# The start of a delta-rule attention and SwiGLU kernel: the first two Gram products, square roots, masks and weight staging rearranged

## The chip, the cores and the metric

The kernel runs on one core of one Trainium2 chip. The metric is the device time of one execution in microseconds (us). Three executions of the kernel before took 696.74, 697.48 and 697.67 us, so the median is 697.48 us. One further execution was profiled. It took 695.99 us, and its span, from the first to the last instruction, is 693.9 us.

## The reference

The input is q, k and v of 4 batches, 8 heads, 768 tokens and 48 values a head, and a scalar beta for every token and head. The first half is a delta-rule recurrence, the second a SwiGLU feed-forward block:

```python
k_n = k / (norm(k, axis=-1) + 1e-06)
for t in range(768):
    y[t]   = q[t] @ state
    v_old  = k_n[t] @ state
    state += beta[t] * outer(k_n[t], v[t] - v_old)
x   = y as (3072 tokens, 384)           # heads side by side
g   = x @ w_gate                        # 384 -> 1536
out = (g * sigmoid(g) * (x @ w_val)) @ w_out   # 1536 -> 384
```

The three weight matrices arrive as 64-bit floats, and are made into 32-bit ones on the chip.

## The kernel before

The recurrence is worked in 12 chunks of 64 tokens. In each chunk, the part that goes through the chunk's own tokens is a triangular system, whose inverse Z comes from the chunk's products K K^T, the norms of k and beta. The kernel makes the inverses for two chunks at a time; the first pair, chunks 0 and 1, has code of its own (the names with `first_`). Four batches are in the tiles as two halves of the 128 partitions, heads as even and odd (`par`).

The start goes so, in the order in which it is written (the order is by hand, each engine works its list from the front, and nothing overtakes on an engine):

- `norms` (VectorE) squares and sums k for chunks 0 and 1. The square root of chunk 0 is a `pow` on GpSimd (L392). For chunk 1, `second_norms` makes it with twelve small VectorE instructions (L399 to L422).
- `turned` transposes k on TensorE, ScalarE copies the result back, and `first_gram` forms K K^T: for chunk 0 in 32 products (L671), for chunk 1 in 64 smaller ones (L677, L678). `first_diag` gathers the 32 by 32 blocks of the diagonal, `spread_beta` brings beta to the rows (L452, L459), `first_scale` multiplies by beta over the square of the norm, partly on GpSimd (L714 to L716), and `first_substitution` inverts by 30 short VectorE instructions (L734, L740). `spread_z` (L757, L759) writes Z where the products read it: for chunk 0 on VectorE and ScalarE, for chunk 1 on GpSimd.
- `gram_steps` makes the products of q and k. For chunks 0 and 1 they are copied by ScalarE and then masked on GpSimd (L566), four instructions of 128x512.
- `stage` loads a piece of the weights. A piece of the first kind is 128 rows by 256 columns of w_gate or w_val, 256 KB. If it is given `after`, GpSimd first copies one column of the earlier piece into the new place (L266), and the load on the SP queue (L267) waits for that copy. So a load starts only when the earlier piece has landed and when GpSimd has come to the copy. Pieces 2 to 13 are held by the piece two before, 14 to 22 by the piece three before. GpSimd's list has the copies of pieces 2 to 5, then the four masks, the two `spread_z` of chunk 1, and then the copies from piece 6 on.
- `power_step` (ScalarE, L279 and L285) and `convert` (VectorE, L296, L304, L316) make the 32-bit weights from a piece that has landed. Both stand in the engines' lists among the work of the attention.
- `first_advance` does the recurrence for chunk 0, `advance(1)` for chunk 1, interleaved with the first feed-forward products by `chain`. `gate_val` (L1477) multiplies by w_gate and w_val: the columns f = 0, 2, 4, 6 (in units of 128, two at a time) for chunk 0, then the same for chunk 1, and so on. f = 0 needs pieces 0 to 5, f = 2 pieces 6 to 11, f = 4 pieces 12 to 17, f = 6 pieces 18 to 23.
- The SP queue holds all loads of this part in one order: q, k, v of the first chunks, pieces 0 to 5, v of chunk 1 (L185), pieces 6 to 22, v of chunk 2, k of chunk 4 (L139), piece 23, and so on.

From chunk 2 on, the feed-forward products go by a scheme with fewer multiplications (L1317, L1594); that part is the same before and after. `unread` issues products whose result nobody reads (L661).

## Time and profile before

| what | before |
|---|---|
| time, median of 3 (lowest, highest) | 697.48 us (696.74, 697.67) |
| time of the profiled execution | 695.99 us |
| its span | 693.9 us |
| TensorE matmul busy | 656.0 us, 95% of the span |
| VectorE, ScalarE, GpSimd busy | 473.2, 255.4, 206.7 us |
| mean granted clock of TensorE | 0.992 |

The span begins with the first instruction, and 2.1 us of the profiled time lie outside it. In rows of instructions ("the timeline") the columns are the start in us, the length from the first start to the last end in us, the engine, the line, the operation, what it writes and reads, the shape and the count; in brackets stands the idle time of the engine just before, and what ended it. PE is TensorE, PEld its weight loads, DVE VectorE, ACT ScalarE, POOL GpSimd, SPq the issue of DMAs by the SP queue. One fp32 product makes two rows of PE and two of PEld, a "pair" each. "issue" means that the engine waited for nothing that the profile shows. In rows of waits the columns are the total in us, the number and the longest. The chain of waits lists start, length and work, following back from the last instruction of the span.

### The profile page before, as it was taken

The page shows a single profiled execution, that of the slowest core. Times are in us where ns is not written, and L with a number is a line of the kernel's source. Part 1 is how long each engine was busy: PE and PEld are TensorE (multiplying, and loading weights), DVE is VectorE, ACT ScalarE, POOL GpSimd, SP SyncE. Part 2 cuts the span into 40 slices and gives each one's busy share as a digit, 9 for nine tenths or more (in the row PEclk, how much of TensorE's full clock was granted, in tenths as well). Part 3 has the DMA queues.
Part 4 walks back from the last instruction along what each step waited for, and adds up shares of the span by engine and source line. Part 5 has one row for each costly group of instructions (what it writes and reads, how often), then busy time and mean ns, then how long its engine had stood idle before and what let it go on. Part 6 is the DMA issues. An engine that isn't in the chain of part 4 may idle for free.

```text
span 693.9 us, 24970 instructions
## 1 busy us (share of the span) xinstructions
PE 656.0 (95%) x10914; PEld 604.4 (87%) x10914; DVE 473.2 (68%) x986; ACT 255.4 (37%) x545; POOL 206.7 (30%) x320
## 2 busy tenths in 40 slices
PE   7877899999899999999999999999999999999997
PEld 4666788856798899999999999999999999999997
DVE  6887478898669956757756757756757755645463
ACT  3876476303532343244233244233222333142130
POOL 6332021203786030783030783030783000000000
PEclk9999899999999999999999999999999999999999
DMA  9645926005314462068172077152077232132220
GB/s 138 159 119 163 258 91 205 1 24 90 97 26 122 113 142 78 19 136 178 39 154 78 14 142 177 37 132 79 15 153 155 64 94 78 40 93 77 70 76 24
DMA packets 147437, 68.57 MB, mean 99 GB/s; under 512 B 123456, under 2 KB 126560, under 8 KB 147328
## 3 DMA queue, kind: packets, MB, share of 16 engines
q1 hardware_dynamic: 144992, 66.48, 40.0%
q8 instruction: 86, 1.41, 0.9%
q10 hardware_dynamic: 2080, 0.39, 0.4%
q14 instruction: 23, 0.19, 0.1%
q0 software_dynamic: 256, 0.10, 0.1%
HBM read 59.08 MB, written 7.86 MB: 96 GB/s over the span
## 4 chain that ended last, share of the span: by engine, by line
PE 75%; DVE 12%; DMA 4%; SPq 3%; issue 2%; POOL 2%; ACT 1%; DVEq 0%; POOLq 0%; ACTq 0%
PE ffn L1317 38%; PE ffn L1594 17%; PE ffn L1477 9%; DMA h_f<-in_moe_w_val_dram 2%; PE p_px L1110 1%; SPq L139 1%; DVE zb L616 1%; DVE x_t L610 1%; PE p_py L527 1%; PE p_py L1164 1%; PE p_px L1091 1%; SPq L185 1%; DVE x_t L1547 1%; PE p_py L1189 1%; PE p_py L1081 1%
## 5 line engine op out<-in xcount | busy, mean ns | idle before, releaser
L1317 PE MATMUL ffn<-x_t,w_gv 128*128 128x128 f32 x760 | 101.5, 277 | 6.7 <-DVE x_t L1544 6.7
L1317 PEld LDWEIGHTS ffn<-x_t,w_gv 128*128 128x128 f32 x760 | 92.3, 192 | 8.4 <-issue 6.1
L1594 PE MATMUL ffn<-wo_sb,h_f 128*128 128x192 f32 x480 | 84.2, 329 | 0.6 <-ACT ffn L1586 0.6
L850 POOL TENSOR_TENSOR n_b<-mb,half 128x32 f32<-128x32 f32 x5 | 27.6, 5526 | 182.2 <-DVE mb L581 182.2
L1317 PE MATMUL ffn<-x_ffn,w_gv 128*128 128x128 f32 x600 | 79.2, 275 | 0.0
L1594 PEld LDWEIGHTS ffn<-wo_sb,h_f 128*128 128x128 f32 x480 | 77.8, 190 | 1.6 <-ACT ffn L1586 0.9
L1353 ACT ACTIVATE sil<-ffn 128x256 f32<-128x256 f32 x95 | 34.6, 382 | 114.9 <-PE ffn L1317 107.0
L616 POOL TENSOR_TENSOR zb<-zb,h_f 128x31 f32<-128x31 f32 (+15 forms) x124 | 72.4, 584 | 9.7
L610 POOL TENSOR_TENSOR h_f<-zb,mb 128x31 f32<-128x31 f32 (+15 forms) x124 | 69.9, 563 | 14.4 <-DVE mb L598 5.0
L1317 PEld LDWEIGHTS ffn<-x_ffn,w_gv 128*128 128x128 f32 x600 | 73.0, 192 | 0.0
L1317 PE MATMUL ffn<-x_t,h_f 128*128 128x128 f32 x464 | 63.6, 280 | 4.2 <-DVE ffn L1544 3.9
L1354 DVE TENSOR_TENSOR h_f<-sil,ffn 128x256 f32<-128x256 f32 x95 | 37.6, 418 | 42.8 <-ACT sil L1353 42.8
L1317 PEld LDWEIGHTS ffn<-x_t,h_f 128*128 128x128 f32 x464 | 56.3, 192 | 6.2 <-DVE ffn L1544 4.9
L1477 PE MATMUL ffn<-x_ffn,w_gv 128*128 128x256 f32 x216 | 48.0, 381 | 0.0
L1477 PEld LDWEIGHTS ffn<-x_ffn,w_gv 128*128 128x128 f32 x216 | 40.7, 190 | 5.6
L1547 DVE TENSOR_TENSOR o_sb<-o_sb,ffn 128x192 f32<-128x192 f32 x49 | 17.1, 349 | 31.4 <-PE ffn L1594 31.0
L1594 PE MATMUL ffn<-last_k,h_f 128*128 128x192 f32 x200 | 35.9, 327 | 0.0
L1477 PE MATMUL ffn<-x_t,w_gv 128*128 128x256 f32 x144 | 35.0, 393 | 0.7 <-DVE x_t L1058 0.7
L1547 DVE TENSOR_TENSOR ffn<-ffn,p_sb 128x512 f32<-128x512 f32 x36 | 24.7, 693 | 16.0 <-PE ffn L1317 14.9
L1594 PEld LDWEIGHTS ffn<-last_k,h_f 128*128 128x128 f32 x200 | 32.8, 190 | 0.2 <-DVE o_sb L1547 0.2
L1477 PEld LDWEIGHTS ffn<-x_t,w_gv 128*128 128x128 f32 x144 | 27.2, 196 | 5.0 <-ACT x_t L1058 0.9
L1317 PE MATMUL ffn<-x_ffn,h_f 128*128 128x128 f32 x224 | 30.0, 277 | 0.0
(351 smaller groups left out, 1178.8 us busy)
## 6 DMA issues: line engine op xcount, KB each, us to landing
h_f<-w_s SPq DMA_DIRECT2D x81, 256.0 KB, 2.8
more_w<-w_s SPq DMA_DIRECT2D x27, 256.0 KB, 2.8
vin<-in_v_dram SPq DMA_DIRECT2D x48, 96.0 KB, 3.5
out_dram<-o_sb SPq DMA_DIRECT2D x48, 96.0 KB, 2.2
kn<-in_k_dram SPq DMA_DIRECT2D x20, 192.0 KB, 4.7
w_s<-h_f SPq DMA_DIRECT2D x10, 256.0 KB, 2.7
zt<-in_moe_w_out_dram SPq DMA_DIRECT2D x6, 384.0 KB, 5.4
qpad<-in_q_dram SPq DMA_DIRECT2D x36, 64.0 KB, 2.9
```

The lines of the kernel that those rows point to most:

```text
L139: dmas[b % len(dmas)].dma_start(out=t[64 * b : 64 * b + 64, :, :, 0:D].rearrange("p bp h d -> p (bp h) d"), in_=halves(x, c, b).rearrange( ...
L185: nc.sync.dma_start(out=vin[c][s : s + 64, par].rearrange("p bp j d -> p (bp j) d"), in_=src[par],)
L527: nc.tensor.matmul(p_v[par][half_of(b if of_q else b ^ par), bp, j], kt[c][half_of(par), bp, j, b], xt[half_of(par), bp, j, b],)
L610: engine.tensor_tensor(out=t_v, in0=zb[:, 0 : j + 1, j : j + 1].to_broadcast([128, j + 1, m]), in1=mb[:, j : j + 1, j + 1 : R].to_broadcas ...
L616: engine.tensor_tensor(out=zb[:, 0 : j + 1, j + 1 : R], in0=zb[:, 0 : j + 1, j + 1 : R], in1=t_v, op=ALU.add,)
L850: nc.gpsimd.tensor_tensor(out=n, in0=mb.rearrange("p j i -> p (j i)")[:, 0 : R * R : R + 1], in1=half, op=ALU.pow,)
L1317: nc.tensor.matmul(p[:, u], w(u), moving, start=start and u == 0, stop=True, skip_group_check=True,)
L1353: nc.scalar.activation(silu_of, p[:, 0:2], ACTF.Silu)
L1354: nc.vector.tensor_tensor(out=h_of(c, PAIRS[r][e % 3], e // 3), in0=silu_of, in1=p[:, 2:4], op=ALU.mult)
L1477: nc.tensor.matmul(ps[name][:, i], w_sb[:, t, (f + i) * 128 : (f + i + 1) * 128], xts[c][:, t], start=(t == 0 and i == 0), stop=(t == KT - 1),
L1547: nc.vector.tensor_tensor(out=out, in0=a, in1=b, op=ALU.add)
L1594: nc.tensor.matmul(p[x, part], a(f - f % 2)[:, f % 2], b(f), start=not begun and f == 0, stop=f == FH - 1, skip_group_check=True,)
```

## The change

- The square root of chunk 1 is now a second `pow` on GpSimd; the twelve VectorE instructions are gone. `first_n` squares the reciprocal, so that beta is multiplied once, on VectorE, and the sign goes into two `scalar_tensor_tensor` of `first_scale`. The transposition of the diagonal blocks stands before `first_n`, not behind it.
- `first_gram` does chunk 1 in 32 products like chunk 0, and `first_diag` combines its two halves like those of chunk 0: two scaled copies on ScalarE and two instructions on VectorE.
- GpSimd's masks of chunk 0 stand between the copies of pieces 6 and 7 and of pieces 7 and 8. The masks of chunk 1 go to VectorE, into the fourth and fifth step of `chain`. Z of chunk 1 is spread by VectorE (first half) and ScalarE (second half) inside `first_advance`.
- Pieces 6 to 9 are held by the piece two before, 10 to 17 by the piece three before, and 18 to 22 by none.
- In `first_advance` the transpositions of y stand before the products for the state. The conversions of pieces 0, 2 and 4 and the power steps of 0, 2, 4 and 1 stand one step of `first_advance` earlier or later than before.

The order of the SP queue is the same before and after. Of the diff, only the body of the removed function is cut:

```diff
@@ -387,39 +387,8 @@
             nc.vector.tensor_reduce(
                 out=n[:, par], in_=ksq_v[:, par], axis=mybir.AxisListType.X, op=ALU.add
             )
-        if c == 0:
-            n = n_t[0][:, c]
-            nc.gpsimd.tensor_tensor(out=n, in0=n, in1=half[:, 0:HH], op=ALU.pow)
-
-    def second_norms():
-
-        n = n_t[0][:, 1]
...
-        nc.vector.tensor_tensor(out=n, in0=n, in1=x, op=ALU.mult)
+        n = n_t[0][:, c]
+        nc.gpsimd.tensor_tensor(out=n, in0=n, in1=half[:, 0:HH], op=ALU.pow)
 
     def divide_beta(g, r_n):
         for _ in range(2):
@@ -463,6 +432,7 @@
         nc.vector.tensor_scalar_add(n, n, 1e-6)
         r_n = work.tile([128, R], FP32, name="r_n", tag="n_b", bufs=1)
         nc.vector.reciprocal(r_n, n)
+        nc.vector.tensor_tensor(out=r_n, in0=r_n, in1=r_n, op=ALU.mult)
         r_b = work.tile([128, R], FP32, name="r_b", tag="nb", bufs=1)
         nc.vector.transpose(r_b, r_n)
         return r_b
@@ -559,8 +529,8 @@
         if of_q and c < 2:
             for par in range(2):
                 to = p_sb[c][:, par].rearrange("p bp j i -> p (bp j) i")
-                under_mask(nc.gpsimd, to, to)
-            yield
+                under_mask(nc.gpsimd if c == 0 else nc.vector, to, to)
+                yield
 
     def under_mask(engine, to, of):
         engine.tensor_tensor(
@@ -663,28 +633,16 @@
     def first_gram(c, tag):
 
         p_v = [p.rearrange("p (x h i) -> p x h i", x=2, i=R) for p in banks("p_g", tag)]
-        half_rows = C
         for bp, j, par, b, _ in every():
             k_v = kt[c][half_of(par), bp, j, b].rearrange("p (x i) -> p x i", x=2)
-            h = NJ * bp + j
-            if c == 0:
-                nc.tensor.matmul(
-                    p_v[par][half_of(b), :, h], kt[c][half_of(par), bp, j, b], k_v
-                )
-                continue
-            hi, lo = QUADS[2 * b][0], QUADS[2 * b + 1][0]
-            twice = k_v[:, 0:1].to_broadcast([half_rows, 2, R])
-            nc.tensor.matmul(p_v[par][hi, :, h], k_v[:, 0], twice)
-            nc.tensor.matmul(p_v[par][lo, :, h], k_v[:, 1], k_v)
+            nc.tensor.matmul(
+                p_v[par][half_of(b), :, NJ * bp + j], kt[c][half_of(par), bp, j, b], k_v
+            )
         return p_v
 
     def first_diag(c, p):
         to = first_of["diag"][:, HH * c : HH * c + HH]
         to = to.rearrange("p (par h) j -> p par h j", par=2)
-        if c > 0:
-            for par in range(2):
-                nc.scalar.copy(to[:, par], p[par][:, 1])
-            return
         for par in range(2):
             nc.scalar.mul(to[:, par], p[par][:, 0], m_rows[:, 3:4])
         for par in range(2):
@@ -709,16 +667,19 @@
 
     def first_scale(r_b):
         zb, b = first_of["zb"], beta_b[:, 0]
-        nb = sil[:, 0, 0:R]
-        for _ in range(2):
-            nc.gpsimd.tensor_tensor(out=b, in0=b, in1=r_b, op=ALU.mult)
-        nc.gpsimd.tensor_scalar_mul(nb, b, -1.0)
+        nc.vector.tensor_tensor(out=b, in0=b, in1=r_b, op=ALU.mult)
         nc.gpsimd.tensor_copy(zb[:, 0 : R * R : R + 1], b)
         mb = pairs_of_blocks(first_of["mb"])[:, :, :, 0:B16]
-        nb = nb.rearrange("p (b i) -> p b i", b=2)[:, :, None, :]
-        nc.vector.tensor_tensor(
-            out=mb, in0=mb, in1=nb.to_broadcast([128, 2, B16, B16]), op=ALU.mult
-        )
+        for x in range(2):
+            at = slice(B16 * x, B16 * x + B16)
+            nc.vector.scalar_tensor_tensor(
+                out=mb[:, x],
+                in0=mb[:, x],
+                scalar=-1.0,
+                in1=b[:, None, at].to_broadcast([128, B16, B16]),
+                op0=ALU.mult,
+                op1=ALU.mult,
+            )
 
     def first_substitution():
 
@@ -1028,6 +989,7 @@
                 lambda par, b, j: t[there(par, b), 1 - par, bp, j],
             )
             plus(uu[:, :, bp], t[:, 1:3, bp], pairs[bp])
+        spread_z(1, 0, nc.vector)
         load_v(2)
         yield
         y = work.tile([128, NB, NJ, 2, D], FP32, name="y", tag="r", bufs=2)
@@ -1042,7 +1004,6 @@
             copy(y[:, bp, :, 0], pairs[bp][:, 0])
             for b in range(2):
                 copy(y[half_of(b), bp, :, 1], pairs[bp][half_of(1 - b), 1])
-        p_s = of_state(0, uu)
         yield
         y_f = y.rearrange("p bp j par d -> p bp (j par d)")
         xts[0] = x_first
@@ -1056,6 +1017,8 @@
                 at = slice(k * 128, (k + 1) * 128)
                 nc.tensor.transpose(p_f[bp][:, k], y_f[:, bp, at], ident)
             copy(x_v[:, :, bp], p_f[bp])
+        p_s = of_state(0, uu)
+        spread_z(1, 1, nc.scalar)
         nc.scalar.copy(state, p_s)
         yield
 
@@ -1865,14 +1828,13 @@
         turned(0, False, 0)
         p_g = [first_gram(0, "px")]
         first_diag(0, p_g[0])
-        second_norms()
         turned(1, False, 2)
         p_g.append(first_gram(1, 2))
         first_diag(1, p_g[1])
         spread_beta(copy_a)
         turned(0, True, 0)
+        nc.vector.transpose(first_of["mb"][:, 0 : R * R], first_of["flat"])
         r_b = first_n()
-        nc.vector.transpose(first_of["mb"][:, 0 : R * R], first_of["flat"])
         first_scale(r_b)
         for n in range(6):
             stage(n, n - 2 if n > 1 else None)
@@ -1899,32 +1861,35 @@
         spread_z(0, 1, nc.vector, others)
         scale_v(0)
         next(first_q[1])
-        power_step(0)
-        next(first_q[1])
+        stage(6, 4)
         next(first_q[0])
-        for x in range(2):
-            spread_z(1, x, nc.gpsimd)
-        for n in range(6, 14):
+        stage(7, 5)
+        next(first_q[0])
+        for n in range(8, 10):
             stage(n, n - 2)
-        for n in range(14, 23):
+        for n in range(10, 18):
             stage(n, n - 3)
+        for n in range(18, 23):
+            stage(n)
         zb_1 = work.tile([128, R, R], FP32, name="zb", bufs=1)
         new_nt(0, spare_of_q, state.rearrange("p b bp j d -> p (b bp j d)")[:, 0:512])
         new_nt(1, zb_1.rearrange("p k i -> p (k i)"), spare_of_q[:, 0:512])
         gens["advance", (0,)] = [first_advance(), 0]
         step("advance", advance, 0)
+        power_step(0)
+        step("advance", advance, 0)
         converts_first(0)
-        step("advance", advance, 0)
-        step("advance", advance, 0)
         power_step(2)
         step("advance", advance, 0)
         converts_first(2)
-        step("advance", advance, 0)
         power_step(4)
         step("advance", advance, 0)
         step("advance", advance, 0)
+        power_step(1)
+        step("advance", advance, 0)
+        step("advance", advance, 0)
         converts_first(4)
-        for n in (1, 3, 5):
+        for n in (3, 5):
             power_step(n)
         scale_v(1)
         converts_first(1)
@@ -1941,6 +1906,8 @@
             step("advance", advance, 1)
             n, ahead = ((1, 7), (2, 6), (4, 4))[len(went)] if len(went) < 3 else (2, 4)
             went.append(n)
+            if len(went) in (4, 5):
+                next(first_q[1])
             convert(todo[:n], ahead)
             del todo[:n]
```

More of the change, by code (lines that the diff above doesn't have):

```diff
@@ L389, in norms @@
             )
-        if c == 0:
-            n = n_t[0][:, c]
-            nc.gpsimd.tensor_tensor(out=n, in0=n, in1=half[:, 0:HH], op=ALU.pow)
-    def second_norms():
-        n = n_t[0][:, 1]
-        x = work.tile([128, HH], FP32, name="x", tag="n_b", bufs=1)
-        t = work.tile([128, HH], FP32, name="t", tag="nb", bufs=1)
-        nc.vector.tensor_scalar(
-            out=words(t),
-            in0=words(n),
-            scalar1=1,
-            scalar2=None,
-            op0=ALU.logical_shift_right,
-        )
-        nc.vector.tensor_scalar(
-            out=words(x),
-            in0=words(t),
-            scalar1=-1.0,
-            scalar2=float(0x5F3759DF),
-            op0=ALU.mult,
-            op1=ALU.add,
-        )
-        for _ in range(3):
-            nc.vector.scalar_tensor_tensor(
-                out=t, in0=x, scalar=-0.5, in1=n, op0=ALU.mult, op1=ALU.mult
-            )
-            nc.vector.tensor_tensor(out=t, in0=t, in1=x, op=ALU.mult)
-            nc.vector.scalar_tensor_tensor(
-                out=x, in0=t, scalar=1.5, in1=x, op0=ALU.add, op1=ALU.mult
-            )
-        nc.vector.tensor_tensor(out=n, in0=n, in1=x, op=ALU.mult)
+        n = n_t[0][:, c]
+        nc.gpsimd.tensor_tensor(out=n, in0=n, in1=half[:, 0:HH], op=ALU.pow)
     def divide_beta(g, r_n):
```

2 lines of the change are left out of this document (removed).

## The prediction

> **What bounds the kernel now.** I read the busy time by stretches first, then the chain of waits, then the timeline of each engine up to 90 us. The stretches have, behind the window, the busy time of PE, PEld, DVE, ACT and POOL, then the granted clock, the DMA share and GB/s.
>
> ```profile
> 60.00:70.00 10.00, 6.43 (x147) 5.31 (x147) 7.06 (x21) 6.93 (x18) 1.15 (x5) 0.89 0.66 201
> 70.00:80.00 10.00, 6.93 (x30) 6.08 (x30) 4.47 (x14) 4.58 (x11) 0.00 (x0) 0.77 1.05 227
> 80.00:90.00 10.00, 10.00 (x166) 8.72 (x165) 7.15 (x14) 6.67 (x13) 0.00 (x0) 1.00 1.02 326
> 90.00:100.00 10.00, 10.00 (x48) 8.81 (x47) 4.92 (x7) 9.91 (x15) 0.00 (x0) 1.00 0.01 3
> ```
>
> TensorE is the bound of the whole. From 80 us on it is busy without a hole (10.00 of 10), but between 60 and 80 us 13.4 of 20, at a lower clock. What the start saves before 78 us therefore moves the end one for one. These are the holes of TensorE:
>
> ```profile
> 62.88 1.56 PE L1477 MATMUL ffn<-x_t,w_gv 128*128 128x256 f32 x6
> 68.00 1.54 PE L1189 MATMUL p_py<-ident,y 128*128 128x128 f32 x6 [3.56 <-ACT y L1179]
> 69.34 2.40 PE L1477 MATMUL ffn<-x_t,w_gv 128*128 128x256 f32 x6
> 74.81 1.94 PE L511 MATMUL p_px<-ident,kn 128*128 128x128 f32 x8 [3.07 <-DVE zt L296]
> 78.16 5.35 PE L1477 MATMUL ffn<-x_t,w_gv 128*128 128x256 f32 x24
> ...
> 121.83 1.04 PE L511 MATMUL p_px<-ident,kn 128*128 128x128 f32 x8
> ```
>
> There is one of 3.56 us ahead of the transpositions of y, and one of 3.07 us ahead of those of k of chunk 4. The rows around them are slow: six products of L1477 take 2.40 us where they took 1.56, and two lots of eight transpositions fill 74.81 to 78.16, where one lot takes 1.04 later. What held them is in ScalarE's and SP's rows:
>
> ```profile
> 62.20 0.45 ACT L279 ACTIVATE w_gv<-wo_sb 128x256 f32<-128x256 f32 x1
> 65.38 0.43 ACT L279 ACTIVATE w_gv<-wo_sb 128x256 f32<-128x256 f32 x1 [2.40 <-DMA wo_sb<-in_moe_w_gate_dram]
> 66.51 0.47 ACT L1177 COPY y<-p_py 128x384 f32<-128x384 f32 x1
> 66.99 0.96 ACT L1179 COPY y<-p_py 64x384 f32<-64x384 f32 x2
> ...
> 29.05 0.33 SPq L267 DMA_DIRECT2D h_f<-in_moe_w_gate_dram  x1
> 31.27 2.64 SPq L185 DMA_DIRECT2D vin<-in_v_dram  x4
> 39.33 0.34 SPq L267 DMA_DIRECT2D h_f<-in_moe_w_gate_dram  x1
> 69.44 1.31 SPq L139 DMA_DIRECT2D kn<-in_k_dram  x2
> ...
> kn<-in_k_dram SPq DMA_DIRECT2D x8, 192.0 KB, 4.8
> h_f<-in_moe_w_gate_dram SPq DMA_DIRECT2D x5, 256.0 KB, 3.4
> ```
>
> ScalarE stood 2.40 us at L279 until a piece of weights had landed, and the copies of y come behind it in its list. The k of chunk 4 was issued at 69.44 and 70.1, which with the median of 4.8 us gives 74.9: the row at 74.81 names VectorE, but it was this load. It was late because the SP queue issues in order and stood for the pieces ahead of it. Why these were late shows on GpSimd:
>
> ```profile
> 30.19 4.96 POOL L566 TENSOR_TENSOR p_sb<-p_sb,mask_q 128x512 f32<-128x512 f32 x4
> 35.13 4.04 POOL L759 TENSOR_SCALAR zt<-mb,m_rows 128x512 f32<-128x512 f32 x2
> 51.92 3.30 POOL L266 COPY wo_sb<-zt 128x1 uint32<-128x1 uint32 x2 [2.38 <-DMA zt<-in_moe_w_val_dram]
> ...
> 35.15 4.02 POOL zt L759 x2
> ```
>
> Piece 4, issued at 29.05, has landed by 32.5 (3.4 us, the median). Its successor, piece 6, was issued at 39.33: the copy that releases it was behind 9.0 us of masks and Z. The last row is of the chain of waits: it runs through Z, and on through the loads behind it.
>
> **The change, part by part.** The sum is made against the profiled execution, 695.99 us, which is 1.5 below the median of 697.48; I carry the difference over to the median.
>
> *Up to the first product of the inverse (L767).*
>
> ```profile
> 11.29 0.18 DVE L399 TENSOR_SCALAR t<-n_t 128x16 uint32<-128x16 uint32 x1
> 13.59 0.17 DVE L422 TENSOR_TENSOR n_t<-n_t,x 128x16 f32<-128x16 f32 x1
> 17.44 0.69 DVE L719 TENSOR_TENSOR wo_sb<-wo_sb,sil 128x512 f32<-128x512 f32 x1 [1.63 <-POOL sil L715]
> 7.94 2.93 POOL L392 TENSOR_TENSOR n_t<-n_t,half 128x16 f32<-128x16 f32 x1 [0.43 <-DVE n_t L387]
> 12.43 0.83 PE L452 MATMUL p_py<-wo_sb,ident 16*32 16x192 f32 x7
> 14.91 1.08 PE L452 MATMUL p_py<-wo_sb,ident 16*32 16x192 f32 x9 [1.64 <-issue]
> 17.06 1.91 PE L511 MATMUL p_py<-ident,kn 128*128 128x128 f32 x8
> 28.04 0.92 PE L527 MATMUL p_px<-qt,kt 64*64 64x64 f32 x45 [1.45 <-issue]
> 30.73 1.16 PE L767 MATMUL ffn<-zt,a_sb 64*64 64x64 f32 x64
> q8 instruction: 86, 1.41, 0.9%
> ```
>
> The twelve instructions (11.29 to 13.76, 2.5 us) go. The second `pow` costs GpSimd 2.93 by the first one's row, so it ends at 13.8, and nothing else waits in GpSimd's list. VectorE gets two combining instructions (0.65 each, as for chunk 0) and two short ones of 0.17. VectorE waited 1.63 us at 17.44 for beta, which was late because TensorE stood in the middle of L452 (12.43 to 14.91). The rows count 222 pairs up to there, 251 to the stall at 28.04. 21,828 instructions of TensorE over 86 instruction packets are 254 a packet, so I read these stalls as places in the instruction list, one every second packet. With 64 pairs fewer ahead, the place falls behind L452, into the first q product. The beta then comes at 13.3. VectorE's own work then brings the scaling (L719, 17.44 to 18.13) to 17.44 - 1.63 - 2.47 + 1.29 + 0.34 = 15.0, and about 0.9 later, because the second pair of combining instructions waits for ScalarE's two scaled copies: 15.9, with two scalings of 0.43 in place of one of 0.69 it ends at 16.8. If beta comes as late as before, it ends at 17.4. So the inversion starts 0.7 to 1.3 earlier. On TensorE the transpositions at 17.06 start up to 1.6 us earlier and at full clock (1.91 against 1.1), and ScalarE, which copies for them without a pause until 28, moves with them. L767 can start up to 2.6 earlier, at 28.1; the stall that stood at 28.04 falls 64 pairs later, into L767 itself, for up to 1.5. Range 0.7 to 2.6; I take **2.0**.
>
> [...]
>
> *`first_advance`, up to the first L1477.*
>
> ```profile
> 41.25 1.15 PE L941 MATMUL p_px<-uu,kn 64*64 64x48 f32 x64 [0.59 <-ACT y L1044]
> 43.94 1.73 PE L1477 MATMUL ffn<-x_t,w_gv 128*128 128x256 f32 x6 [0.74 <-DVE x_t L1058]
> ```
>
> The state products (1.15) no longer stand between y and its transpositions: up to 1.1 gained. Against that stand Z on VectorE (128x512; a mask of that size takes 0.68, below), ScalarE's power steps (two of 0.43 to 0.45, above) ahead of copies, 0.5 where they don't fit a gap, and the stalls with "issue", which come as fast as before per pair while the work is moved up. From -1 to +1.5; **+0.3**.
>
> *Chunk 1, 43.94 to 64.44.*
>
> ```profile
> 60.47 0.55 DVE L1547 TENSOR_TENSOR uu<-qpad,p_px 128x384 f32<-128x384 f32 x1 [0.15 <-ACT qpad L1149]
> 61.08 0.94 PE L941 MATMUL p_px<-uu,kn 64*48 64x48 f32 x64
> 85.94 0.68 DVE L566 TENSOR_TENSOR p_sb<-p_py,mask_q 128x512 f32<-128x512 f32 x1
> ```
>
> TensorE is full here, and nothing is removed. VectorE gets two masks, 0.68 each by the row at 85.94. The first lies ahead of the adder at 60.47, whose end (61.02) releases L941 at 61.08: no slack, so 0.6 is lost. The second is covered by L941 (0.94) before L1164 reads it. **-0.6**, from -1.5 to 0.
>
> *The loads.* Piece 6 is released at 32.7, but SP issues v of chunk 1 until 33.9: 34.0 for 39.33. Each further link takes a landing (3.4) and a copy (0.2): piece 8 at 37.6, 11 at 41.2, 14 at 44.8, 17 at 48.4. A mask of chunk 0 (1.24) between two copies hides in the landing; y of chunk 0 reads it at 39. Pieces 18 to 22 wait for nobody and are issued by 50.5. v of chunk 2 (2.6 of issue) and k of chunk 4 follow on SP: 54.5 for 69.44. ScalarE took piece 17 at 62.20 and 18 at 65.38; moved up by 2, and without the wait, they are due near 58 and 59, and they land at 52 and 53. So the hole of 3.56 closes: the copies of y, 1.4 us, follow the products of p and u, which end before the last row of L1477 does (64.44). I take **3.0**, since they stand behind a sigmoid and a power step. The hole of 3.07 closes wholly: **3.1**. With the holes the slow rows go: 2.40 to 1.56, 1.54 to 1.1, 3.35 to 2.1: 2.5 at most; **1.7**. Next late is VectorE: it is busy 7.06 of the 10 us from 60 to 70, and gets two masks and Z more, 2.0 us, for less time.
>
> Sum: 2.0 + 0.3 - 0.6 + 3.0 + 3.1 + 1.7 = 9.5. Profiled 686.5, median **688.0**. Later loads are issued on conversions, which move up as well, and between 90 and 100 us the DMAs were idle; so nothing takes it back.
>
> **The rivals.**
>
> *VectorE or ScalarE become the bound before 78 us.* The conversions of pieces 12 to 17 must be done before f = 4. For it: VectorE's 7.06 of 10 and the 2.0 us more; against it: its 4.47 from 70 to 80, work that may come after the 24 products of f = 4. If half of the 7.8 us from holes and slow rows comes back as waiting, the gain is 5.6, with a worse start 4: 691.9 to 693.5.
>
> *The loads were hidden anyway.* Then only the first three parts count, 1.7: 695.8. Against it stand the 2.40 us of ScalarE and the load at 69.44.
>
> *GpSimd's copies are held by VectorE: slower.* Of the two copies at 51.92 the second came after 2.57 us without a reason in the profile, and ended as VectorE's unbroken run did (55.06):
>
> ```profile
> 54.65 0.41 DVE L316 CUSTOM_DVE_ANT_0 w_gv<-w_gv,last_h 128x512 uint16<-128x512 uint16 x1
> ```
>
> VectorE now has more to do in that time. Five copies stand in series, from piece 6 (by 8, 11 and 14) to piece 17. At 2.6 each, piece 17 is issued at 61.4 instead of 48.4, lands at 64.8, and ScalarE, which took it at 62.2 before, is 2.6 late; with 1.7 saved at the start and the pieces behind in a bunch, about 1 slower: 698.5. It decides from about 2 us a copy on; of 21 copies one showed it. [...]
>
> **How the numbers follow.** Forecast (7 to 12 us gained) 0.67; VectorE or ScalarE the bound 0.18; loads hidden 0.08; copies held 0.07, of which 0.05 slower and 0.02 no change. Below 0.2% (1.4 us) this kernel's measurement tells nothing. Faster 0.93, same 0.02, slower 0.05. The upper end is 693.0, the second case's; the lower 685.0, where the first part gives 2.6, the second 1 and the slow rows 2.5 (12.5 in all).
>
> **What the next profile would show.** L767 near 28.7; piece 6 issued at 34; no wait of ScalarE for a weight DMA between 50 and 66; k of chunk 4 issued by 56; the 24 products of f = 4 at 68 to 69 instead of 78.16, and TensorE full from there. It is wrong if a new wait of some us stands ahead of f = 4 or if the GpSimd copies have gaps of 2 us.

## The result, and the profile after

The kernel after took 690.03 us (median of 4 runs, 687.16 to 692.41) beside 697.11 us for the kernel before (4 runs, 696.31 to 697.67): a ratio of 0.9898, with a 95% interval from 0.9858 to 0.9937, or 7.1 us gained. The profiled execution took 689.76 us, its span is 688.1 us. The runs of the kernel after lie 5 us apart, those of before 1.4; why, is part of the story below.

The busy time by stretches of the kernel after, columns as in the prediction:

```profile
60.00:70.00 10.00, 7.66 (x144) 6.60 (x142) 6.51 (x20) 4.71 (x12) 0.00 (x0) 0.66 0.90 201
70.00:80.00 10.00, 10.00 (x174) 8.88 (x173) 7.43 (x20) 6.63 (x15) 0.00 (x0) 1.00 0.92 240
80.00:90.00 10.00, 10.00 (x48) 8.81 (x47) 6.81 (x13) 9.84 (x18) 0.00 (x0) 1.00 0.39 154
```

TensorE is now full from 70 us on instead of 80. Between 60 and 70 it is not: 7.66 of 10 us busy, and that at a granted clock of 0.66, lower than before (0.89). The timeline of TensorE in the kernel after:

```profile
27.78 1.30 PE L728 MATMUL ffn<-zt,a_sb 64*64 64x64 f32 x64 [0.21 <-ACT zt L718]
31.82 0.49 PE L932 MATMUL p_px<-v,qpad 64*64 64x48 f32 x18 [1.02 <-issue]
35.82 0.49 PE L932 MATMUL p_px<-x_t,qpad 64*64 64x48 f32 x18 [1.02 <-issue]
41.18 1.56 PE L1440 MATMUL ffn<-x_t,w_gv 128*128 128x256 f32 x6
...
57.95 1.56 PE L1440 MATMUL ffn<-x_t,w_gv 128*128 128x256 f32 x6
59.87 0.94 PE L902 MATMUL p_px<-uu,kn 64*48 64x48 f32 x64 [0.36 <-DVE uu L1510]
60.62 0.74 PE L1127 MATMUL p_py<-uu,p_sb 64*64 64x48 f32 x34
63.70 1.10 PE L1127 MATMUL p_py<-uu,p_sb 64*64 64x48 f32 x30 [2.34 <-issue]
64.73 2.93 PE L1440 MATMUL ffn<-x_t,w_gv 128*128 128x256 f32 x6
67.45 1.49 PE L1152 MATMUL p_py<-ident,y 128*128 128x128 f32 x6
68.73 1.95 PE L1440 MATMUL ffn<-x_t,w_gv 128*128 128x256 f32 x6
70.52 1.04 PE L481 MATMUL p_px<-ident,kn 128*128 128x128 f32 x8
71.39 1.04 PE L481 MATMUL p_py<-ident,qpad 128*128 128x128 f32 x8
72.26 5.35 PE L1440 MATMUL ffn<-x_t,w_gv 128*128 128x256 f32 x24
```

Both old holes (3.56 and 3.07 us) are gone: the transpositions of y (L1152) and of k of chunk 4 (L481) come without a wait. In their place stands a new one, in the middle of the products of P and U (L1127): after 34 of its 64 products TensorE stands 2.34 us, and no engine and no transfer is named, only "issue". Behind it six products that take 1.56 us elsewhere take 2.93. The 24 products of f = 4 start at 72.26 instead of 78.16, 5.90 us earlier, and from there to the end both profiles take the same time (688.05 - 72.26 = 615.8, 693.92 - 78.16 = 615.8). So all that the change did happened ahead of that row.

The loads of the kernel after, from the timelines of SP, GpSimd and VectorE:

```profile
30.64 2.64 SPq L185 DMA_DIRECT2D vin<-in_v_dram  x4
33.37 1.24 SPq L267 DMA_DIRECT2D h_f<-in_moe_w_gate_dram  x1
46.43 1.20 SPq L267 DMA_DIRECT2D wo_sb<-in_moe_w_gate_dram  x1
52.99 0.33 SPq L267 DMA_DIRECT2D wo_sb<-in_moe_w_val_dram  x1
56.91 2.87 SPq L185 DMA_DIRECT2D vin<-in_v_dram  x4
59.87 3.73 SPq L139 DMA_DIRECT2D kn<-in_k_dram  x2
...
48.97 4.00 POOL L266 COPY wo_sb<-wo_sb 128x1 uint32<-128x1 uint32 x1 [2.57 <-DMA wo_sb<-in_moe_w_gate_dram]
...
52.51 0.41 DVE L316 CUSTOM_DVE_ANT_0 w_gv<-w_gv,last_h 128x512 uint16<-128x512 uint16 x1
```

Piece 6 goes out at 33.37 (39.33 before), piece 16 at 46.43, but piece 17 only at 52.99: the copy that releases it, of one column, took 4.00 us on GpSimd and ended as VectorE's unbroken run did (52.92). Pieces 18 to 22, which wait for nobody but stand behind it in SP's queue, then follow within 3.4 us (53.63 to 56.36), v of chunk 2 from 56.91 and k of chunk 4 at 59.87, ten us earlier than before.

Last, the same stretch of the kernel after cut where the granted clock changes:

```profile
59.47:62.88 3.41, 1.53 (x99) 1.37 (x98) 3.41 (x9) 1.39 (x4) 0.00 (x0) 1.00 0.90 198
62.88:66.30 3.42, 2.60 (x34) 2.24 (x35) 3.42 (x13) 1.37 (x3) 0.00 (x0) 0.50 0.73 151
66.30:69.71 3.41, 3.41 (x13) 2.85 (x12) 0.21 (x1) 2.18 (x7) 0.00 (x0) 0.50 1.07 277
69.71:73.12 3.41, 3.41 (x25) 3.17 (x24) 2.33 (x7) 3.41 (x11) 0.00 (x0) 1.00 0.52 90
```

In all 14 profiles the clock is 1.00 or 0.50, and the stretches between its changes last multiples of 3.41 us; a window below is one such 3.41 us. Here it fell to half at 62.88, at the end of a stretch in which TensorE was busy 1.53 of 3.41 us, and came back at 69.71, at the end of one in which it was busy throughout (3.41 of 3.41). Counted over the whole windows of the 14 profiles that began at the full clock, the clock fell after every one with less than 1.65 us of TensorE busy and after none with more than 2.05; in between both occur: in the kernel before the clock fell after a window of 1.77 us and not after one of 1.80, in the kernel after not after one of 1.95.

### The profile page after: what moved, and what is told of

The parts are those of the page before. It is cut to its first block, busy times and chain, and to the rows that moved or that the text cites. A ratio compares the mean times of both kernels' runs of the same rounds, so it can differ in the third digit from the quotient of the medians.

```text
span 688.1 us, 24813 instructions
## 1 busy us (share of the span) xinstructions
PE 653.7 (95%) x10850; PEld 603.7 (88%) x10850; DVE 473.3 (69%) x982; ACT 256.1 (37%) x546; POOL 201.7 (29%) x309
## 4 chain that ended last, share of the span: by engine, by line
PE 64%; DVE 3%; issue 0%; DVEq 0%
PE ffn L1280 36%; PE ffn L1557 17%; PE p_px L1073 1%; PE p_px L1054 1%; PE p_py L497 1%; PE p_py L1127 1%; PE p_py L1044 1%; DVE x_t L1510 1%; DVE ffn L1507 1%; PE p_px L902 1%; PE p_px L497 1%; PE p_py L1152 1%; PE p_py L884 1%; PE p_px L870 1%; DVE o_sb L1510 0%
## 5 line engine op out<-in xcount | busy, mean ns | idle before, releaser
L1440 PEld LDWEIGHTS ffn<-x_ffn,w_gv 128*128 128x128 f32 x216 | 40.7, 190 | 5.6
```

The costliest lines, as they stand in the source:

```text
L1440: nc.tensor.matmul(ps[name][:, i], w_sb[:, t, (f + i) * 128 : (f + i + 1) * 128], xts[c][:, t], start=(t == 0 and i == 0), stop=(t == KT - 1),
```

## The experiments

TensorE's instructions come in packets of 16 KB: the kernel after has 85 of them for 21,700 rows of TensorE, by these numbers 255 instructions each. A block is what one packet holds, and a fetch is its transfer. Theory one, formed from these rows: a fetch of TensorE's instructions that falls into a burst of loads comes late; the stall of 2.34 us belongs to a place in the instruction list, and the slow clock follows from it. And for the gain: the loads carry it. The rivals are named with each run. All times are against runs of the kernel before on the same chip, whose medians lay between 696.94 and 698.13 us, so kernels are compared by their ratios.

One table for all of them; the parts below refer to it. "N" is the first product of the inverse (n_products), "stall" is the longest idle time of TensorE with "issue" between 46 and 66 us, "wait for k" the idle time ahead of the transpositions of k of chunk 4, "half clock" the time at a clock of 0.5 ahead of the products of f = 4, all in us and from the profile of each. The profiled execution is one of the runs and not always a typical one: in after_2 and conv_back it was the slowest (693.71 and 691.76 us).

| kernel | N starts | k of chunk 4 issued | stall | wait for k | half clock | f = 4 starts | median | ratio, 95% interval |
|---|---|---|---|---|---|---|---|---|
| before | 30.73 | 69.44 | 0.38 | 3.07 | 10.2 | 78.16 | 697.1 | |
| after | 27.78 | 59.87 | 2.34 | 0 | 6.8 | 72.26 | 690.03 | 0.9898 (0.9858 to 0.9937) |
| after_2 | 31.39 | 58.41 | 2.58 | 0 | 20.5 | 75.38 | 688.67 | 0.9880 (0.9846 to 0.9915) |
| after_3 | 28.17 | 54.71 | 1.71 | 0 | 20.5 | 74.65 | 690.38 | 0.9920 (0.9878 to 0.9962) |
| start_only | 27.75 | 69.16 | 0.34 | 4.24 | 8.4 | 77.59 | 696.25 | 0.9969 (0.9950 to 0.9988) |
| rest_only | 30.98 | 58.48 | 0.91 | 0 | 10.2 | 71.02 | 690.38 | 0.9895 (0.9875 to 0.9915) |
| tail_held | 28.00 | 61.02 | none | 0 | 13.7 | 70.01 | 688.05 | 0.9863 (0.9840 to 0.9886) |
| tail_held_2 | 28.74 | 57.64 | 0.25 | 0 | 10.2 | 70.45 | 687.88 | 0.9871 (0.9838 to 0.9903) |
| shift_64 | 31.18 | 57.69 | 0.52 | 0 | 13.7 | 71.86 | 690.17 | 0.9887 (0.9868 to 0.9907) |
| holds_before | 28.25 | 62.30 | 1.21 | 0 | 13.7 | 72.05 | 691.36 | 0.9899 (0.9873 to 0.9924) |
| z_on_pool | 27.82 | 61.76 | 1.77 | 0 | 10.2 | 72.23 | 689.27 | 0.9896 (0.9864 to 0.9928) |
| free_from_14 | 27.84 | 53.30 | 2.26 | 0 | 13.7 | 73.12 | 691.13 | 0.9896 (0.9871 to 0.9920) |
| loads_before | 29.03 | 67.81 | 0.57 | 5.77 | 17.9 | 77.24 | 695.75 | 0.9982 (0.9958 to 1.0006) |
| conv_back | 28.20 | 55.33 | 2.31 | 0 | 10.2 | 73.26 | 687.94 | 0.9882 (0.9844 to 0.9921) |

From f = 4 to the end every one of them takes 615.2 to 617.2 us.

### The two halves of the change: start_only and rest_only

start_only is the kernel before with the new first K K^T, the square roots on GpSimd and the new first_scale; rest_only is the kernel before with everything else.

```
# start_only: of the diff, these parts alone
+        n = n_t[0][:, c]
+        nc.gpsimd.tensor_tensor(out=n, in0=n, in1=half[:, 0:HH], op=ALU.pow)
...
-        second_norms()
# rest_only: of the diff, all but first_gram, first_diag, norms, first_n and first_scale
```

> The kernel before with the start of the change alone (first K K^T in 32 products, square roots of chunk 1 on GpSimd, the new first_scale); masks, Z of chunk 1, loads and conversions as before. If the parts add up (theory one), N starts 2.5 to 3 us earlier, the two holes of 3.56 and 3.07 us stay, and the time falls by 2 to 3 us, to 694 to 695. If the loads alone set when the products of f=4 start (rival), the start's gain is swallowed by a longer hole and the time stays within 0.7 us of 697.

> The kernel before with all of the change but its start. Its TensorE list has the 64 pairs of the old first K K^T, so a place in the list where TensorE fetches anew lies 64 pairs earlier in the work of chunk 1 than in the kernel after. Theory one (the 2.34 us of stall in the P U products of chunk 1 belong to the place in the list, reached while the weights' DMAs hold up the fetch, and the slow clock of 62.9 to 69.7 us follows from it): N starts at 30.7, but that stall is under 1.2 us, no slow clock before 75 us, and the time is 687 to 690. Rival (the stall belongs to the P U products or to their operands): stall and slow clock stay, and the time is 691 to 694.

start_only gained 0.31% (2.2 us), as theory one had it in time, but not in its way: N started 3.0 us earlier, and f = 4 only 0.6. The holes did not stay; one grew. In the timeline of TensorE of start_only:

```profile
68.45 1.46 PE L1438 MATMUL ffn<-x_t,w_gv 128*128 128x256 f32 x6
74.15 1.94 PE L481 MATMUL p_px<-ident,kn 128*128 128x128 f32 x8 [4.24 <-DMA kn<-in_k_dram]
```

k of chunk 4 is issued at 69.16, as late as before, so an earlier start waits for it longer. In its profile the rival is nearer to the truth; by its runs a gain of 0.1 to 0.5% is left. rest_only reached 0.9895, the same as the whole change, with an N that starts 3.2 us later:

```profile
30.98 1.16 PE L767 MATMUL ffn<-zt,a_sb 64*64 64x64 f32 x64
...
64.54 1.11 PE L1166 MATMUL p_py<-uu,p_sb 64*64 64x48 f32 x64
65.58 1.56 PE L1479 MATMUL ffn<-x_t,w_gv 128*128 128x256 f32 x6
```

The products of P and U run through at full clock, as theory one expected; no slow clock stands between 46.00 and f = 4. So the halves do not add: alone the start is worth some 2 us, on top of the rest nothing that these runs can tell.

### The place in the instruction list: shift_64

```
-        unread(2, banks("p_t", 2)[0])
+        p_w = banks("p_t", 2)[0]
+        for _ in range(34):
+            nc.tensor.matmul(p_w[0:R, 0:32], half, half[:, 0:1].to_broadcast([128, 32]))
```

> The kernel after with the two 512-column products of the second unread() cut into 34 of 32 columns: TensorE as long busy there, while it waits for the substitution, but 64 pairs more stand in its list, and nothing else is changed. Theory one (the stall belongs to a place in the list): by the kernel after's own trace the blocks then begin where it had 54.99 and 60.28 us; the stall of 2.34 us in the P U products goes, one of 0.3 to 0.9 us comes ahead of the state's products at about 60.3, the clock stays full up to 78 us, and the time is 684 to 686.5. Rival (operands or a bank of these products): the stall stays at 2 to 2.5 us at the same products and the time within 1 us of the kernel after.

The timeline of TensorE in shift_64:

```profile
59.69 0.25 PE L1098 MATMUL p_px<-uu,qpad 64*64 64x48 f32 x1 [0.52 <-issue]
...
65.38 1.11 PE L1127 MATMUL p_py<-uu,p_sb 64*64 64x48 f32 x64
66.42 1.56 PE L1440 MATMUL ffn<-x_t,w_gv 128*128 128x256 f32 x6
```

The stall left the products of P and U, and one of 0.52 us came where the block now begins, as theory one had it. Nothing but products whose result nobody reads was changed, and 40 us earlier, so neither operands nor a bank caused it. The list says the same by itself: numbered from the first, the stalls with "issue" of 0.25 us and more between 26 and 66 us, in the eleven profiles whose list has 10,850 pairs of weight load and product, stand at pairs 599, 727, 982, 1110, 1238 and 1494 (one less or more), which are multiples of 128 apart: 128 pairs are 256 instructions.

The fetch was late here too: the block begun at 53.77 had its packet 3.63 us later, at 57.40. But TensorE runs on for 5.4 us in this block before it stands, and for 3.9 in the one of the kernel after that begins at 57.49. So what a late fetch costs depends on what stands in its block.

The time did not fall: 690.17 us, and here theory one missed by 3.7. In this profile N starts at 31.18 instead of 27.78, since the clock was at half from 19.27 to 29.51; the narrow products may have caused it, but after_2 shows the same (19.71 to 29.95) without them. From N to f = 4 shift_64 takes 40.7 us, the kernel after 44.5, 44.0 and 46.5 in its three profiles.

### The burst of loads: tail_held, free_from_14, tail_held_2 and after_3

```
 # tail_held and tail_held_2
-        for n in range(10, 18):
+        for n in range(10, 23):
             stage(n, n - 3)
-        for n in range(18, 23):
-            stage(n)
 # free_from_14
-        for n in range(10, 18):
+        for n in range(10, 14):
             stage(n, n - 3)
-        for n in range(18, 23):
+        for n in range(14, 23):
             stage(n)
```

> The kernel after with pieces 18 to 22 held by copies as before. Theory one (the burst of pieces 18 to 22 at 53 to 57 us holds up the instruction fetch): the fetch that began 3.62 us after its block's first product now begins within 2.2 us, the stall in the P U products is under 1.2 us, and the time falls below 688 unless k of chunk 4 comes so late that its transposes wait. Rival (the copies on GpSimd, in series behind unbroken runs of VectorE, set the loads): each of the five costs 1 to 3 us, k of chunk 4 is issued at 65 to 70 us, its transposes wait 2 to 5 us, and the time is 691 to 696.

> The kernel after with pieces 14 to 17 not held either, so that no copy on GpSimd is held by VectorE's run and the burst of loads comes some 5 us earlier. Theory one (a fetch of instructions that falls into a burst of loads starts late): the late fetch (over 3 us after its block's first product) moves from the block begun at 57.5 to one begun at 48 to 53 us, the stall in the P U products is under 1.2 us, and the time is 686 to 689. Rival (the copy held 4.0 us delayed k of chunk 4 and the conversions, and that is what the kernel after lost): the same gain, but the fetch lags stay under 2.2 us at every block. Third (neither matters): the stall stays and the time is 689 to 691.

The timeline of TensorE in tail_held:

```profile
62.57 0.94 PE L902 MATMUL p_px<-uu,kn 64*48 64x48 f32 x64 [0.36 <-DVE uu L1510]
63.33 1.32 PE L1127 MATMUL p_py<-uu,p_sb 64*64 64x48 f32 x64
64.58 1.56 PE L1440 MATMUL ffn<-x_t,w_gv 128*128 128x256 f32 x6
```

No stall and no slow clock stand there, and k of chunk 4, behind five more copies, was issued at 61.02 and still not waited for. The time, 688.05, is at the bound that theory one gave. The rival is out. The fetches themselves are in the trace. The table has, for each profile, the block ahead of the longest stall (in tail_held the block in the same place as in the kernel after): when it begins, from when to when the next packet is transferred, and when the next block begins.

```
                 block begins  packet from  to      next block begins  stall
after            57.49         61.11        62.25   63.70              2.34
after_2          52.99         55.91        57.91   59.28              2.58
after_3          51.48         54.85        55.73   57.22              1.71
conv_back        52.59         55.98        57.21   58.60              2.31
free_from_14     46.36         49.90        50.78   52.26              2.26
tail_held        60.20         61.64        62.58   63.98              none
```

The next block begins 1.4 to 1.5 us after its packet has ended. What differs is the start of the packet: 2.9 to 3.6 us after the block where the stall is long, 1.4 in tail_held (1.1 to 2.0 at the other blocks of the kernel after between 28 and 57 us). And the bursts differ: in these five profiles pieces 18 to 22 are not held and leave within a few us. In the six profiles with the list of 10,850 pairs and that tail free the longest stall is 1.7 to 2.6 us, in the five with it held 0 to 1.2. With 64 pairs more in the list and the tail free, as in shift_64 and rest_only, it is 0.52 and 0.91. In free_from_14 the burst came earlier (k of chunk 4 at 53.30) and the stall with it, to 52.26, as theory one had it; but the stall stayed as long and the time, 691.13, did not fall, which it had not expected. No copy on GpSimd was held there longer than 0.81 us, and yet the fetch lagged 3.54 us, so the second case is out too: the copy that was held 4.00 us in the kernel after cost nothing that shows.

For the time, the kernel after and tail_held were run once more, side by side:

> The kernel after with pieces 18 to 22 held as before, once more, beside the kernel after itself. Theory one (the burst of the five unheld pieces holds up a fetch of instructions; without it the stall of the P U products goes): no stall over 1.2 us between 58 and 66 us, and a median 0.5 to 2.5 us below that of the kernel after. Rival (the first run's lead was chance): a median within 0.5 us of it, or above.

> The kernel after, unchanged, beside the three others. By its earlier runs: a median of 688.5 to 690.5 us, single runs up to 5 us apart, and a granted clock that is lower where the time is longer.

tail_held_2 took 687.88 us (686.37 to 689.32) and after_3 690.38 (687.99 to 693.16); the means differ by 3.0 us, with a standard error of 0.8 (6 and 7 runs). Theory one's expectation came in, at the upper end of its size: holding the tail takes the stall away and is faster. That the stall itself makes the difference in time is not shown. The mean granted clock of the seven runs of after_3 was 0.9861, of the six of tail_held_2 0.9907. As an estimate, time times mean clock is the time at full clock: 681.3 and 681.4 us. By this the whole lead is slow clock; that the stall brings the slow clock about is argued from the windows above, not shown. Of all that was run, holding these five pieces as before is the only edit whose lead over the kernel after is outside the scatter side by side (conv_back, below, leads by 2.2 in the means, with a standard error of 1.2). The stall of after_3, in its timeline of TensorE, shows that even the place is not fixed, since the loads come at other times from run to run:

```profile
54.49 1.02 PE L1098 MATMUL p_px<-v,zb 64*64 64x48 f32 x52 [0.25 <-ACT v L1081]
57.22 0.67 PE L1098 MATMUL p_px<-v,zb 64*64 64x48 f32 x12 [1.71 <-issue]
```

The kernel after had been run a second time already:

> The kernel after, unchanged, run again beside the three that follow, since its four runs lay 5 us apart. Theory one (its stall in the P U products is part of its instruction list and of its loads): the stall comes again within 1.5 to 2.6 us and the time is 689 to 691, a ratio of 0.988 to 0.991. Rival (a chance of one execution): the stall is gone and the time lies below 688.

It came out as theory one had it in time (688.67) and in the size of the stall (2.58), but at another block, as in after_3. Over the 17 runs of the kernel after, the six at a mean granted clock of 0.983 or 0.984 took 690.4 to 693.7 us, mean 692.4, the eleven at 0.987 to 0.992 686.1 to 692.4, mean 689.0. So most of its scatter goes with the clock.

### What brought the loads forward: z_on_pool, holds_before, loads_before and conv_back

z_on_pool puts masks and Z of chunk 1 back on GpSimd ahead of the copies; holds_before gives pieces 8 to 22 their old holds; loads_before does both; conv_back puts conversions and power steps back in the old order. The edits are shown shortened: on the way back, the copies of pieces 6 and 7 stand behind masks and Z again, and the masks leave `chain`.

```
 # z_on_pool and loads_before (and the two spread_z(1, ...) of first_advance taken out)
+        next(first_q[1])
+        next(first_q[1])
         next(first_q[0])
         next(first_q[0])
+        for x in range(2):
+            spread_z(1, x, nc.gpsimd)
 # holds_before and loads_before
-        for n in range(8, 10):
+        for n in range(8, 14):
             stage(n, n - 2)
-        for n in range(10, 18):
+        for n in range(14, 23):
             stage(n, n - 3)
-        for n in range(18, 23):
-            stage(n)
```

> The kernel after with every hold of pieces 8 to 22 as before (8 to 13 on the piece two back, 14 to 22 on the piece three back), Z and masks of chunk 1 as after. Theory one (the loads came early because Z and masks left GpSimd's queue, not because of the holds): the products of f=4 start at 69 to 71.5 us and the time is 686 to 689. Rival (the looser holds carried the gain): pieces 10 to 13 come 1 to 2 us later each, k of chunk 4 after 64 us, f=4 starts after 73 us and the time is 691 to 695.

> The kernel after with both masks and both halves of Z of chunk 1 on GpSimd ahead of pieces 6 to 22, as before; start, holds and conversions as after. Theory one (the 10 us of GpSimd's work ahead of the copies was what kept the weights back): piece 6 is issued at 36 to 40 us instead of 33.4, waits of 2 us or more for weights or k of chunk 4 stand again ahead of f=4, which starts after 75 us, and the time is 693 to 696. Rival (holds and the order of conversions carried the gain): f=4 starts before 73.5 us and the time is 688 to 691.

For holds_before theory one was right on f = 4 (72.05, half a us late) and k of chunk 4 (62.30), but the time, 691.36, lies in the range of the rival; the ratio, 0.9899, is close to the 0.9898 and 0.9880 of the kernel after, so the gain is kept and neither expectation fits whole. z_on_pool contradicts theory one outright: 689.27. In its timeline of SP:

```profile
40.64 0.33 SPq L267 DMA_DIRECT2D h_f<-in_moe_w_gate_dram  x1
58.48 0.43 SPq L267 DMA_DIRECT2D zt<-in_moe_w_gate_dram  x1
61.76 3.12 SPq L139 DMA_DIRECT2D kn<-in_k_dram  x2
```

Piece 6 leaves at 40.64, later than in the kernel before, and yet piece 22 leaves at 58.48, because with the looser holds the pieces behind catch up. So neither half of the loads' part (Z and masks off GpSimd, looser holds) is needed while the other is there. Two readings were left: each is enough alone, or neither matters and the order of conversions does it.

> The kernel after with masks and Z of chunk 1 on GpSimd ahead of pieces 6 to 22 and with every hold as before; its start, the later place of the state's first products and the order of its conversions stay. Theory one (either Z off GpSimd or the looser holds is enough, as the two kernels with only one of them undone showed; k of chunk 4 has to be issued by about 64 us): with both undone k of chunk 4 is issued after 66 us, waits of over 2 us stand ahead of f=4, which starts after 75 us, and the time is 693 to 697. Rival (the order of conversions carried the gain): f=4 starts before 73.5 us and the time is 688 to 691.5.

> The kernel after with the conversions and power steps of first_advance in the order of before; loads, masks, Z and start as after. Theory one (the loads carry the gain, and the order of conversions takes no part that ends last): the time lies within 1.5 us of the kernel after, 688 to 691. Rival (the order of conversions carried it): f=4 starts 3 us later or more and the time is 692 to 696.

conv_back lost nothing (687.94), so the order of conversions carries no gain. With both halves undone the gain is gone, 0.9982 with 1 inside the interval, and k of chunk 4, f = 4 and the time came as theory one said. The timelines of TensorE and SP in loads_before:

```profile
66.57 1.46 PE L1438 MATMUL ffn<-x_t,w_gv 128*128 128x256 f32 x6
73.80 1.94 PE L481 MATMUL p_px<-ident,kn 128*128 128x128 f32 x8 [5.77 <-DMA kn<-in_k_dram]
...
67.81 1.31 SPq L139 DMA_DIRECT2D kn<-in_k_dram  x2
```

The early start runs into a hole of 5.77 us. By the table, k of chunk 4 is not waited for where it is issued by 62.3, and waited for by 3 us and more where it is issued at 67.8 or later. No run lies between the two. Issuing it at 53 or 55 brings nothing further that shows.

## Why the prediction was right, and where not

The forecast was 688.0 us, 9.5 us gained; measured are 690.03 and 7.1, in the range and of the right sign, and the mechanism (earlier loads close both holes ahead of f = 4) is what the runs show. In the profiled pair f = 4 moved by 5.90 us. That the time came as near as it did is in part luck: two steps of the sum came out worse than their bounds (`first_advance` in the other profiles, chunk 1 in this one), and N came better than its range. The prediction's signs of being wrong stood in the profile too, "a new wait of some us" ahead of f = 4 (2.34 us) and a GpSimd copy held for more than 2 us (4.00), while the holes closed all the same. By the steps of the prediction:

| step | forecast | profiled pair |
|---|---|---|
| up to the first product of N | 2.0 | 2.95 (30.73 to 27.78) |
| first_advance | +0.3 | -0.2 (13.21 to 13.40 us long) |
| chunk 1 and the hole of 3.56 | -0.6 + 3.0 | -2.2 (43.94 to 68.00 was 24.06, 41.18 to 67.45 is 26.27) |
| hole of 3.07 and slow rows | 3.1 + 1.7 | 5.35 (68.00 to 78.16 was 10.16, 67.45 to 72.26 is 4.81) |
| sum | 9.5 | 5.9 |

*Up to N.* The right mechanism, and a size above its range. Of the twelve profiles with the new start ten have N between 27.75 and 29.03, against 30.73 and 30.98 with the old one; the two others had the clock at half from 19 to 30. Its bound of 2.6 has no sum: the terms named for it, 1.6 us and 0.8 for the full clock, give 2.4. The stall that it put into the products of the inverse, up to 1.5 us, did not come there; in the kernel after they take 1.30 us in place of 1.16. That the stalls with "issue" are places in the instruction list is shown by shift_64. Two parts of that reading were wrong: they come at every 128 pairs, not at every second packet, and a stall that is moved does not go. The next ones stand at 31.82 and 35.82, 1.02 us each.

*first_advance is a step that failed,* though it is within its bounds in this profile. In the eleven other profiles with the new order of `first_advance` the stretch takes 14.55 to 17.01 us, so it loses 1.3 to 3.8 us against the 13.21 before, where at most 1 was allowed. In after_3 it took 16.24 us (28.17 to 44.41), and the clock was at half from 36.44 to 46.68. tail_held shows how that comes; its stretches, cut where the clock changes:

```profile
32.68:36.09 3.41, 1.68 (x80) 1.34 (x78) 3.34 (x6) 2.77 (x9) 2.63 (x3) 1.00 0.65 122
36.10:46.34 10.24, 9.44 (x190) 8.01 (x190) 6.56 (x15) 5.96 (x15) 1.29 (x6) 0.50 0.64 186
```

TensorE was busy 1.68 of 3.41 us, between stalls and waits, and 10.24 us at half clock followed. No term of the sum stood for that.

*Chunk 1 is the other step that failed:* "TensorE is full here, and nothing is removed". The mask on VectorE cost 0.36 us at 59.87, where 0.6 was put, and the hole of 3.56 closed. But 2.34 us of stall and 1.37 us of slow products (2.93 for 1.56) came in, with 0.5 to 0.6 us at each of the two block starts at 44.34 and 48.61. The sum gave 2.4 us for this stretch and it lost 2.2; the difference, 4.6 us, is more than the whole miss of the profiled pair. It comes again: the stretch takes 25.68 and 26.48 us in after_2 and after_3, and 22.09 and 22.63 in tail_held and tail_held_2, where the sum had 21.7. So the cause lies in the step on the loads: "Pieces 18 to 22 wait for nobody" was counted as gain alone. Where they are let go at once TensorE's next block comes late, and by tail_held they were not needed that early.

*Both holes and the slow rows* came as said, the rows a little better (5.35 for 4.8). Half of the reason given was not needed: "Why these were late shows on GpSimd" is true of the kernel before, but z_on_pool is as fast with those 9 us of GpSimd still in place.

*After f = 4* nothing is taken back, as said.

The rivals: VectorE and ScalarE did not become the bound. In tail_held VectorE is busy without a break from 60 to 70 us, and TensorE's only wait for it is 0.36 us. The loads were not hidden: loads_before shows what they cost. The held copies did occur: one, 4.00 us, more than the 2.57 on which that rival was built. The VectorE instructions beside it take 0.3 to 0.4 us each, so if VectorE held it, it did so across a dozen of them and not for the length of one. It did not decide, because four of the five links in series were free, and the k behind it had 2.4 us to spare by the table (59.87 against 62.3). The lower end of the range has a slip: with the three larger terms the sum is 11.6 us, or 12.2 with chunk 1 at 0, and not 12.5.

What the crossing of a block costs, the same traces show. In the kernel after, between 28 and 57 us, the packet starts 1.1 to 2.0 us after its block begins and takes 0.9 to 1.3, and where TensorE stands for it the next block begins 1.3 to 1.6 us after its end. There three blocks, whose 128 pairs took 3.83, 4.36 and 5.05 us, ended without a stall; four, whose pairs took 2.8 to 3.7 us, ended with one of 0.51 to 1.02 us, and the late packets in the five profiles of the table cost 1.7 to 2.6.

Part of the gain is clock. Over 46 runs the kernel before had a mean granted clock of 0.9844, over 17 the kernel after 0.9878: 10.9 us and 8.4 us of full-speed time lost. So by this estimate about 2.5 of the 7 us are slow clock. Which windows went is not shown: ahead of f = 4 the kernel before has 10.2 us at half clock in its one profile, the kernel after 6.8, 20.5 and 20.5 in its three.

Open stays why a fetch starts late. Each of the long stalls has a burst beside it, but in rest_only the packet beside the burst started after 1.82 us, and which transfer a late one waits for no view shows. Open is also whether the start's 3 us could be kept: with 64 pairs more in the list, as in rest_only and shift_64, the way from N to f = 4 takes 40.0 and 40.7 us, with fewer 41.7 to 46.5 where k of chunk 4 is not waited for. tail_held with a list shifted by products of full width was not run.

## What to carry to other kernels

Before a load is let go earlier, ask from which issue time on its consumer no longer waits, and stop there: here k of chunk 4 was early enough when issued by 62.3 us, two independent edits each achieved it, and going further brought nothing that shows and, with the usual list, a stall of TensorE beside the burst. Where products are short, count pairs in blocks of 128: here, where TensorE stood for the next block between 28 and 50 us, that one began 3.8 to 4.3 us after the one before, and a stall that is moved out of one stretch appears in another. And a stall is priced with the clock behind it, since 1.88 us of idle time in one window of 3.41 us (the kernel after) and 1.73 in another (tail_held) were followed by 6.8 and 10.2 us at half clock.

## What the runs showed of the hardware

- A packet of 16 KB of TensorE's instructions started 1.1 to 2.0 us after its block began at the seven blocks of the kernel after that begin between 28 and 53 us, and 2.9 to 3.6 us after it beside a burst of loads (56 to 58 us in the kernel after: 330 GB/s) in the five profiles of the table; TensorE then stood 1.7 to 2.6 us.
- The granted clock was 1.00 or 0.50 for multiples of 3.41 us, and fell after windows in which TensorE was busy 1.53 (the kernel after) and 1.68 us (tail_held) of 3.41; over 14 profiles it fell after every window below 1.65 us and none above 2.05.
- A copy of one column on GpSimd, 0.18 to 0.96 us elsewhere in the kernel after, took 4.00 us there beside an unbroken run of VectorE, across about a dozen of its instructions.
- The square root of 128x16 values on GpSimd took 2.91 us each in the kernel after.
